# Cached attention on one core: the first V loads moved ahead of K in the load queue, smaller last pieces of wo, and the two output copies exchanged

## The chip, the cores and the metric

The kernel runs on one core of one Trainium2 chip. The metric is the device time of one execution in microseconds (us). A core has five engines: TensorE (PE in the profile; its weight loads are PEld), VectorE (DVE), ScalarE (ACT), GpSimd (POOL) and SyncE (SP), which here only issues transfers. Sixteen DMA engines move the data. A 2 MB load is split over all sixteen, and it has landed when the last of them has finished its share. A landing given without a line of a view is read from the trace's completion counts, sixteen for each load.

## The reference, cut to what matters

```python
# B = 32 batches, 4 queries each, 32 query heads over 4 KV heads, 2048 keys, head size 128, bf16
q = (x @ wq).reshape(B, Sq, Hq, Dh).transpose(0, 2, 1, 3)
scores = einsum("bhqd,bhkd->bhqk", q, repeat(k_cache, 8)) * Dh ** -0.5
o = einsum("bhqk,bhkd->bhqd", softmax(scores), repeat(v_cache, 8))
return o.transpose(0, 2, 1, 3).reshape(B, Sq, Hq * Dh) @ wo
```

Each batch reads 2 MB of K and 2 MB of V once. With wq and wo (8 MB each) that is 151 MB, and little arithmetic on each byte: the time is that of reading.

## The kernel before

All loads go through one list, in one order, from SyncE. There are eight slots of 2 MB in `big`: four for V (slots 0 to 3), three for K (4 to 6), one for another use. The four pieces of wq first lie in the V slots, so no V can be loaded until the q projection has read wq.

```python
NW = 4; LEAD = 3; S2 = 12; VS = 4; KS = 3; LAG = 3
WO = (4, 4, 4, 4, 4, 4, 4, 2, 1, 1)      # heads in each piece of wo; one head is 256 KB

loads = [("k", b) for b in range(LEAD)]
for b in range(B):
    ahead = b + LEAD + (b >= S2)
    ks = [("k", a) for a in range(len(loads) - b, ahead + 1) if a < B]
    loads += ks + [("v", b)]              # K0 K1 K2 | K3 V0 | K4 V1 | K5 V2 ...
# [...]
for kind, b in loads:
    waits = ["qproj"] * (b < VS) if kind == "v" else []
    if kind == "v" and b >= VS:
        waits = [("pv", b - VS)]          # the slot's last V has been used by TensorE
    if kind == "k" and b >= KS:
        waits = [("kt", b - KS, NCH - 1)] # the slot's last K has been transposed by VectorE
    # [...] one DMA of 2 MB on SyncE
```

K3 therefore waits for the transposes of K0, and these come after the q projection. V0 stands behind K3, though all that V0 itself needs is the projection.

At the end the products with wo run piece by piece, and two engines copy the two halves of y out of PSUM, where TensorE has summed them:

```python
for c in range(len(WO)):
    oproj(c)     # per head two matmuls of 128x512, after the wait for piece c
def oproj_out():
    p.op("dve", tensor_copy(y_sb[:, 0:NC], ps_s[:, 0:NC]), [("op", 0)], ("oe", 0))
    p.op("act", activation(y_sb[:, NC:D], ps_s[:, NC:D], ACT.Copy), [("op", 1)], ("oe", 1))
    for j, eng in enumerate(("sp", "act")):
        # [...] eng issues the write of half j after ("oe", j)
```

Of the kernel before, what the change touches and what calls it, by code (L numbers as in the profile page):

```python
# [5 lines left out]
ACT = mybir.ActivationFunctionType  # L6
# [97 lines left out]
def bass_standalone__gqa_block_cached__sampling_kernel(  # L104
# [8 lines left out]
    B, Sq, D = x.shape  # L113
# [11 lines left out]
    NS = 8  # L125
    NW = 4
    LEAD = 3
    S2 = 12
    VS = 4
    KS = 3  # L130
    LAG = 3
    QB = 4
    NC = D // 2
    WO = (4, 4, 4, 4, 4, 4, 4, 2, 1, 1)
    scale = float(Dh) ** -0.5

    x_flat = x.rearrange("b s d -> (b s) d")
# [2 lines left out]
    with ExitStack() as es:  # L140
# [18 lines left out]
        y_sb = P_flat[:, D:2 * D]  # L159
# [8 lines left out]
        ps_s = es.enter_context(nc.psum_tensor("ps_s", [128, Sk], F32))  # L168
# [9 lines left out]
        p = _Program()  # L178
# [7 lines left out]

        loads = [("k", b) for b in range(LEAD)]
        for b in range(B):
            ahead = b + LEAD + (b >= S2)
            ks = [("k", a) for a in range(len(loads) - b, ahead + 1) if a < B]  # L190
            loads += ks + [("v", b)]

        def slot_of(kind, b):
            return b % VS if kind == "v" else VS + b % KS
# [18 lines left out]
        h0 = 0  # L213
        for c, m in enumerate(WO):
            assert h0 // 8 == (h0 + m - 1) // 8
            kind, b = wo_for[h0 // 8]
# [186 lines left out]
        def ot_evac(i):  # L403
            buf = ring_of["ot", i]
            p.op("act", lambda e: e.activation(  # L405
                oT_sb[:, :, :, i * Sq:(i + 1) * Sq].rearrange("p h e s -> p e h s"),
                buf[:, 0:128].rearrange("p (e h s) -> p e h s", e=2, s=Sq), ACT.Copy),
                [("oT", i)], ("ot", i))

        def oproj(c):  # L410
            for h in range(sum(WO[:c]), sum(WO[:c + 1])):
                for j in range(2):
                    out_, lhsT, rhs = ps_s[:, NC * j:NC * (j + 1)], oT_sb[:, h // 2, h % 2, :], wo_at(h, 1)[:, NC * j:NC * (j + 1)]
                    if j == 0:
                        mm = lambda e, a=(out_, lhsT, rhs), h=h: e.matmul(  # L415
                            a[0], lhsT=a[1], rhs=a[2], start=(h == 0), stop=(h == Hq - 1), skip_group_check=True)
                    else:
                        mm = lambda e, a=(out_, lhsT, rhs), h=h: _matmul_held(
                            nc, e, *a, tile_size=(128, 128), tile_position=(0, 0), start=(h == 0), stop=(h == Hq - 1))
                    p.op("pe", mm, [("wo", c), ("ot", B - 1)], ("op", j) if h == Hq - 1 else None)  # L420

        def oproj_out():
            p.op("dve", lambda e: e.tensor_copy(y_sb[:, 0:NC], ps_s[:, 0:NC]), [("op", 0)], ("oe", 0))  # L423
            p.op("act", lambda e: e.activation(y_sb[:, NC:D], ps_s[:, NC:D], ACT.Copy), [("op", 1)], ("oe", 1))  # L424
            for j, eng in enumerate(("sp", "act")):
                p.dma(eng, lambda e, j=j: e.dma_start(out_flat[:, NC * j:NC * (j + 1)], y_sb[:, NC * j:NC * (j + 1)]),
                      [("oe", j)], ("out", j), f"s_o{j}")

# [7 lines left out]
        for i in range(B + LAG):  # L436
            j = i - LAG
# [27 lines left out]
        ot_evac(L)  # L465
        for c in range(len(WO)):
            oproj(c)
        oproj_out()

        p.loop = starts[4:B + 1:4]  # L470
# [55 lines left out]
```

## Time and profile before

| | before |
|---|---|
| median of three runs before the prediction | 365.92 us (365.52 to 366.39) |
| span of the profiled run | 363.9 us |
| moved | 151.7 MB, 417 GB/s over the span |
| busy: TensorE, VectorE, GpSimd, ScalarE | 85%, 76%, 46%, 31% |

The page cuts the span into 40 equal slices. These are the slices of the kernel before, first the DMA engines' busy share in tenths, then what they moved:

```profile
DMA  8999999999999999999999999999999999999994
GB/s 322 432 432 432 391 430 427 427 421 424 429 427 430 430 432 424 423 429 429 430 428 432 428 427 421 429 429 430 430 432 429 425 425 426 429 432 423 403 409 163
```

The stream is full nearly everywhere. Besides the two ends, one slice stands out, the fifth (36 to 45 us, 391 GB/s). This is the timeline of SyncE's queue there; the columns are start, duration, engine and line, operation, destination and source, and the duration is that of the issue, not of the transfer:

```profile
36.05 0.33 SPq L205 DMA_DIRECT2D big<-in_k_cache_dram  x1
36.43 0.43 SPq L205 DMA_DIRECT2D big<-in_v_cache_dram  x1
45.26 0.33 SPq L205 DMA_DIRECT2D big<-in_k_cache_dram  x1
45.62 0.43 SPq L205 DMA_DIRECT2D big<-in_v_cache_dram  x1
```

The first of these is K3. The view of the tile K, narrowed to this one issue, gives its time to landing:

```profile
DMA to landing us min/median/max: 7.7/7.7/7.7
```

So K3 landed at 43.8 us. K2 had landed at 37.88. The regular distance of two 2 MB loads in this trace is 4.89 us, so K3 came 1.04 us late. The windows of 2 us show the same (the last three columns are TensorE's granted clock, the DMA engines' share, and GB/s; a packet is counted where it starts, so a share can exceed 1):

```profile
36.00:38.00 2.00, 2.00 (x11) 0.19 (x2) 1.15 (x2) 0.00 (x0) 0.00 (x0) 1.00 1.14 311
38.00:40.00 2.00, 2.00 (x11) 0.10 (x1) 1.13 (x1) 0.00 (x0) 0.92 (x4) 1.00 0.81 344
```

The chain of work that ended last, in order of time (start, duration, what), shows the tail:

```profile
338.75 18.36 DMA big<-in_wo_dram
357.11 0.05 issue
357.16 0.39 PE ps_s L415
...
360.82 0.60 ACT P_sb L424
```

TensorE's last wait is for the piece of heads 24 to 27, landed at 357.11. From there TensorE alone sets the pace: 16 matmuls, one each 0.216 us. And the last lines of the timeline:

```profile
360.61 0.69 DVE L423 CAST P_sb<-ps_s 128x512 bf16<-128x512 f32 x1 [22.39 <-PE ps_s L415]
360.82 0.60 ACT L424 ACTIVATE P_sb<-ps_s 128x512 bf16<-128x512 f32 x1 [16.26 <-PE ps_s L16]
361.32 0.35 SPq L426 DMA_DIRECT2D out_dram<-P_sb  x1
361.45 0.37 ACTq L426 DMA_DIRECT2D out_dram<-P_sb  x1
```

The first half of y is ready at 360.61 (VectorE starts on it then), 1.02 us after the last byte of wo landed at 359.59. The two writes landed at 363.10 and 363.43.

### The profile page before, as it was taken

Reading aid. Unit: us, or ns where it says so; the run is one execution under the profiler, and the core shown is the slowest. Engines: PE = TensorE matmul, PEld = TensorE weight load, DVE = VectorE, ACT = ScalarE, POOL = GpSimd, SP = SyncE. Lnnn points to the kernel's source line nnn. Section 1 sums busy time; section 2 is a strip of 40 time slices with the busy share of each in tenths; the row PEclk is TensorE's granted clock in tenths of the full one; section 3 lists DMA queues with packets and bytes.
Section 4 is the critical chain, followed back from the end, with each engine's and each line's share of the span. In section 5 each row is a group of like instructions: output and inputs, shape, how many; then the busy total and the mean of one; then the engine's idle time right before and its main releaser. Section 6 shows DMA issues by size and latency. Waiting matters only on the chain. (4 is left out here: it accounts for less than half of the span.)

```text
span 363.9 us, 6546 instructions
## 1 busy us (share of the span) xinstructions
PE 309.2 (85%) x2991; PEld 142.1 (39%) x2402; DVE 275.8 (76%) x275; ACT 111.3 (31%) x142; POOL 165.9 (46%) x261
## 2 busy tenths in 40 slices
PE   1987777899999999998999988888888888989885
PEld 1002000444444444444444444444333334449711
DVE  0028799999999999889999988898888888856100
ACT  1014222333333333333333333333332223333100
POOL 8002155255555555555455544445555555444000
PEclk9999999999999999999999999999999999999999
DMA  8999999999999999999999999999999999999994
GB/s 322 432 432 432 391 430 427 427 421 424 429 427 430 430 432 424 423 429 429 430 428 432 428 427 421 429 429 430 430 432 429 425 425 426 429 432 423 403 409 163
DMA packets 12573, 151.68 MB, mean 417 GB/s; under 512 B 1296, under 2 KB 1552, under 8 KB 3856
## 3 DMA queue, kind: packets, MB, share of 16 engines
q1 hardware_dynamic: 12416, 151.39, 98.5%
q10 hardware_dynamic: 144, 0.13, 0.1%
q8 instruction: 6, 0.10, 0.1%
q14 instruction: 7, 0.06, 0.0%
HBM read 151.26 MB, written 0.26 MB: 416 GB/s over the span
## 5 line engine op out<-in xcount | busy, mean ns | idle before, releaser
L323 DVE STREAM_TRANSPOSE KT_sb<-big 128x1024 f32<-128x1024 f32 x128 | 150.8, 1218 | 10.3 <-DMA big<-in_k_cache_dram 10.3
L350 ACT ACTIVATE P_sb<-ps_s,negmx 128x2048 bf16<-128x2048 f32 x32 | 82.1, 2566 | 86.0 <-DVE negmx L346 86.0
L16 PE MATMUL ps_s<-KT_sb,QD_sb 128*128 128x512 bf16 x384 | 103.7, 377 | 0.0
L372 POOL COPY PD_sb<-PT_sb 32x1024 f32<-32x1024 f32 x62 | 64.2, 1035 | 72.0 <-PE ps_r L383 42.8
L372 POOL COPY big<-PT_sb 32x1024 f32<-32x1024 f32 x61 | 63.7, 1044 | 59.8 <-PE ps_r L383 28.9
L345 DVE TENSOR_REDUCE mx<-ps_s 128x1 f32<-128x2048 f32 x32 | 73.3, 2291 | 10.5 <-PE ps_s L16 9.5
L383 PE MATMUL ps_r<-big 128*128 128x128 bf16 x1024 | 59.8, 219 | 8.7 <-PEq L85 8.6
L383 PE MATMUL ps_r<-big,PD_sb 128*128 128x128 bf16 x1024 | 59.8, 219 | 8.1 <-PEq L85 8.1
L383 PEld LDWEIGHTS ps_r<-big,PD_sb 128*128 128x128 bf16 x1024 | 58.0, 98 | 20.0 <-issue 18.9
L383 PEld LDWEIGHTS ps_r<-big 128*128 128x128 bf16 x1024 | 57.9, 98 | 19.9 <-issue 19.0
L336 PE MATMUL ps_s<-KT_sb,QD_sb 128*128 128x512 bf16 x128 | 48.3, 377 | 17.9 <-PEq L85 17.9
L336 PEld LDWEIGHTS ps_s<-KT_sb,QD_sb 128*128 128x128 bf16 x128 | 12.3, 96 | 103.7 <-issue 103.7
L360 DVE STREAM_TRANSPOSE PT_sb<-P_sb 128x1024 f32<-128x1024 f32 x32 | 39.9, 1246 | 15.1 <-ACT P_sb L350 15.1
L313 POOL COPY QD_sb<-QT_sb 32x64 f32<-32x64 f32 x128 | 29.5, 231 | 38.2 <-DVE QT_sb L292 20.8
L405 ACT ACTIVATE oT_sb<-ps_r 128x128 bf16<-128x128 f32 x32 | 8.9, 278 | 106.6 <-PE ps_r L400 106.6
L16 PE MATMUL ps_r<-QT_sb,ident 128*128 128x512 bf16 x132 | 33.7, 379 | 4.5 <-issue 4.3
L423 DVE CAST P_sb<-ps_s 128x512 bf16<-128x512 f32 x1 | 0.7, 692 | 22.4 <-PE ps_s L415 22.4
L400 PEld LDWEIGHTS ps_r<-ident,o_sb 128*64 128x64 bf16 x128 | 4.6, 109 | 31.2 <-issue 30.9
L390 ACT ACTIVATE o_sb<-ps_r,rinv 128x128 bf16<-128x128 f32 x32 | 11.7, 367 | 15.6 <-PE ps_r L383 13.7
L274 DVE CAST KT_sb<-ps_r 128x512 bf16<-128x512 f32 x2 | 1.3, 685 | 20.1 <-PE ps_r L258 20.1
L415 PE MATMUL ps_s<-big,oT_sb 128*128 128x512 bf16 x30 | 11.4, 380 | 1.6 <-DMA big<-in_wo_dram 1.6
L16 PE MATMUL ps_s<-big,oT_sb 128*128 128x512 bf16 x32 | 12.1, 379 | 0.7 <-ACT oT_sb L405 0.7
(41 smaller groups left out, 86.0 us busy)
## 6 DMA issues: line engine op xcount, KB each, us to landing
big<-in_k_cache_dram SPq DMA_DIRECT2D x32, 2048.0 KB, 17.8
big<-in_v_cache_dram SPq DMA_DIRECT2D x32, 2048.0 KB, 21.5
big<-in_wq_dram SPq DMA_DIRECT2D x4, 2048.0 KB, 14.0
big<-in_wo_dram SPq DMA_DIRECT2D x7, 1024.0 KB, 20.0
big<-in_wo_dram SPq DMA_DIRECT2D x1, 512.0 KB, 17.2
big<-in_wo_dram SPq DMA_DIRECT2D x2, 256.0 KB, 14.8
P_sb<-in_x_dram SPq DMA_DIRECT2D x1, 256.0 KB, 2.7
out_dram<-P_sb SPq DMA_DIRECT2D x1, 128.0 KB, 1.8
```

The source lines that it names most:

```text
L16: return eng.add_instruction(mybir.InstMatmult(name=nc.get_next_instruction_name(), engine=eng.engine, start_tensor_calc=start, stop_tenso ...
L313: p.op("pool", lambda e, s=src, d=dst: e.tensor_copy(d, s), waits if g == 0 else [], ("qd", i) if g == G - 1 else None)
L323: p.op("dve", lambda e, s=src, d=dst: e.transpose(d, s), waits, ("kt", i, c), gives="t_kt" if c == NCH - 1 else None)
L336: mm = lambda e, a_=(out_, lhsT, rhs), f=first, l=last: e.matmul(a_[0], lhsT=a_[1], rhs=a_[2], start=f, stop=l, skip_group_check=True)
L345: p.op("dve", lambda e: e.tensor_reduce(mx[:, i % 4:i % 4 + 1], ps_s[:, :], AX.X, ALU.max), [("qk", i)], ("mx", i))
L350: p.op("act", lambda e: e.activation(P_sb[:, :, :, :].rearrange("p t r w -> p t w r"), ps_s[:, :].rearrange("p (t w r) -> p t w r", w=2, r=R),
L360: p.op("dve", lambda e: e.transpose(dst, src), [("exp", i)] + ([("pd", i - 2, G - 1)] if i > 1 else []), ("pt", i))
L372: p.op("dve" if i >= B - 2 and g < i - B + 4 else "pool", lambda e, s=src, d=dst: e.tensor_copy(d, s), [("pt", i), free], ("pd", i, g))
L383: p.op("pe", lambda e: e.matmul(buf[:, 0:Dh], lhsT=pd_of(i)[:, t // 2, :, :, t % 2].rearrange("p g q -> p (g q)"), rhs=big[:, slot_of("v", ...
L390: p.op("act", lambda e: e.activation(o_sb[:, :], buf[:, 0:Dh], ACT.Copy, scale=rinv[:, i % 4:i % 4 + 1]), [("pv", i), ("rinv", i)] + ([("o ...
L405: p.op("act", lambda e: e.activation(oT_sb[:, :, :, i * Sq:(i + 1) * Sq].rearrange("p h e s -> p e h s"), buf[:, 0:128].rearrange("p (e h ...
L415: mm = lambda e, a=(out_, lhsT, rhs), h=h: e.matmul(a[0], lhsT=a[1], rhs=a[2], start=(h == 0), stop=(h == Hq - 1), skip_group_check=True)
```

## The change

Three small edits: V stands ahead of the next K in the first six batches, so that the queue has work while K3 waits; the last megabyte of wo but one (heads 24 to 27) comes in two pieces, so that TensorE is less behind at the end; and the copies of y are exchanged.

```diff
     LEAD = 3
+    S1 = 6
     S2 = 12
@@
-    WO = (4, 4, 4, 4, 4, 4, 4, 2, 1, 1)
+    WO = (4, 4, 4, 4, 4, 4, 2, 2, 2, 1, 1)
@@
-            loads += ks + [("v", b)]
+            loads += [("v", b)] + ks if b < S1 else ks + [("v", b)]
@@ oproj_out
-            p.op("dve", lambda e: e.tensor_copy(y_sb[:, 0:NC], ps_s[:, 0:NC]), [("op", 0)], ("oe", 0))
-            p.op("act", lambda e: e.activation(y_sb[:, NC:D], ps_s[:, NC:D], ACT.Copy), [("op", 1)], ("oe", 1))
-            for j, eng in enumerate(("sp", "act")):
+            p.op("act", lambda e: e.activation(y_sb[:, 0:NC], ps_s[:, 0:NC], ACT.Copy), [("op", 0)], ("oe", 0))
+            p.op("dve", lambda e: e.tensor_copy(y_sb[:, NC:D], ps_s[:, NC:D]), [("op", 1)], ("oe", 1))
+            for j, eng in enumerate(("act", "sp")):
```

The order becomes K0 K1 K2, V0 K3, V1 K4, V2 K5, V3 K6, V4 K7, V5 K8, then K9 V6 as before.

## The prediction

> **What bounds the kernel now.** The page shows the 16 DMA engines at 0.99 busy or more in almost every fortieth of the span, at 425 to 432 GB/s. The Trainium skill ("HBM Reference", Specifications) gives about 425 GB/s for one core streaming alone; the trace agrees. From 54 us on nearly every 2 MB K or V load lands 4.89 or 4.90 us after the one before. Compute follows. So time can come only from places where the queue is dry, and from what follows the last byte. Three lie near the change:
> 1. Head (queue timeline, windows of 2 us). The loads of wq and K0 to K2 are issued by 4.0 us; K3 waits for K0's transposes and goes out at 36.05, V0 behind it at 36.43. K2 lands at 37.88, K3 at 43.80: 5.93 us instead of 4.89, so 1.04 us lost; windows 36 to 40 show 311 and 344 GB/s. K4, issued at 45.26, lands 0.36 us late likewise.
> 2. Tail (chain of waits). The last wo piece of four heads (24 to 27) lands at 357.11; 16 matmuls of 0.216 us follow, and the first half of y is ready at 360.6. The last piece landed at 359.59, so this is TensorE catching up.
> 3. Output. VectorE copies half 0 (0.69 us, done 361.30, landed 363.10); ScalarE starts half 1 at 360.82 (0.60 us), and its write lands last, at 363.43.
>
> **What the change does.**
> 1. V0 waits only for the q projection (over at about 26.4 us), so it is queued before K2 has landed. K3 is issued at 36.05 as before, now behind 4.9 us of V0: the gap closes, and each later pair has one V more ahead of it. Worth about 1.0 us (0.7 to 1.3: the 16 engines lost 0.72 to 1.03 us each at K3, 0.05 to 0.37 at K4). The price: K3 to K8 stand one V later, about 3.9 us net. Before, K8 landed 4.7 us ahead of its first transpose; about 0.8 is left, so VectorE may wait a little. As loads set the pace, that costs nothing unless the queue runs dry.
> 2. Heads 24 and 25 would land at about 355.83, 26 and 27 at 357.11, 28 and 29 at 358.33, the last as before. TensorE starts its last eight matmuls at 358.38, not at about 358.89: 0.5 us off. No bytes are added; one more issue on a queue 15 us ahead is free.
> 3. The later half gets the slower copy (+0.09 us) but the quicker write (1.78 us from issue to landing against 1.98), the earlier half the reverse: about 0.1 us off.
>
> All three lie on the critical path: 1.0 + 0.5 + 0.1 = 1.6 us, estimated from these durations. 365.92 - 1.6 = 364.3 us, range 363.4 to 365.3. Chances: faster by over 2% 0.02, within 2% 0.97, slower 0.01.
>
> **What would show it right.** V0's issue near 26.6 us; K2, V0, K3 landing 4.9 us apart; all later landings about 1 us earlier; windows 36 to 40 at about 425 GB/s. At the end, TensorE's last wait on wo is for heads 28 and 29, and the first half is done about 1.8 us after they land.
>
> **What would make it wrong.** V in front of K starving VectorE around K5 to K8, so that slots free late and the queue runs dry; single DMA engines held up elsewhere (V1 landed 1.31 us late before, beside an instruction fetch at 57 us), which moves the end by a microsecond either way; or the engine that ends last having lost least in the gap.

## The result, and the profile after

| | before | after |
|---|---|---|
| median, six runs each | 365.87 us (365.52 to 366.84) | 364.33 us (364.26 to 364.40) |
| ratio | | 0.9954 (95%: 0.9941 to 0.9967) |
| the same later, on another chip | 366.20 us (365.95 to 367.30) | 364.43 us (364.33 to 364.63) |
| ratio | | 0.9944 (95%: 0.9929 to 0.9958) |

A ratio is the mean time of one kernel's runs over that of the other's of the same rounds, so it is not quite the ratio of the medians. The verdict is "same" at the 2% line; the gain is about half a per cent, and clear. Not only the middle moved: the kernel before spreads over 1.3 us in both series, the changed one over 0.1 to 0.3 us.

The slices of the changed kernel; the fifth now moves 434 GB/s:

```profile
DMA  7999999999999999999999999999999999999995
GB/s 324 432 430 434 434 423 423 427 430 430 423 425 427 430 430 424 430 425 430 430 426 427 424 432 432 425 427 427 430 432 425 427 427 431 430 427 427 401 407 195
```

SyncE's queue, from 20 us on. V0 goes out at 26.82, nine microseconds ahead of K3:

```profile
26.82 0.33 SPq L206 DMA_DIRECT2D big<-in_v_cache_dram  x1
35.97 0.33 SPq L206 DMA_DIRECT2D big<-in_k_cache_dram  x1
36.34 0.43 SPq L206 DMA_DIRECT2D big<-in_v_cache_dram  x1
45.17 0.33 SPq L206 DMA_DIRECT2D big<-in_k_cache_dram  x1
```

K3's time to landing, in the same narrowed view, and the windows:

```profile
DMA to landing us min/median/max: 11.6/11.6/11.6
```

```profile
36.00:38.00 2.00, 2.00 (x11) 0.19 (x2) 1.07 (x1) 0.00 (x0) 0.00 (x0) 1.00 1.04 442
38.00:40.00 2.00, 2.00 (x11) 0.10 (x1) 1.22 (x1) 0.00 (x0) 0.93 (x4) 1.00 0.94 401
```

K2 landed at 37.78, V0 at 42.67, K3 at 47.57: 4.89 and 4.90 us apart. K3 waits longer in the queue, and nothing waits for K3. The mean of the two windows is 421 GB/s, against 327 before.

The chain now ends with the piece of heads 28 and 29, and eight matmuls behind it:

```profile
341.77 15.61 DMA big<-in_wo_dram
357.38 0.04 issue
357.42 0.39 PE ps_s L416
...
359.36 0.69 DVE P_sb L425
```

```profile
359.14 0.60 ACT L424 ACTIVATE P_sb<-ps_s 128x512 bf16<-128x512 f32 x1 [15.56 <-PE ps_s L416]
359.36 0.69 DVE L425 CAST P_sb<-ps_s 128x512 bf16<-128x512 f32 x1 [22.14 <-PE ps_s L16]
359.77 0.37 ACTq L427 DMA_DIRECT2D out_dram<-P_sb  x1
360.08 0.35 SPq L427 DMA_DIRECT2D out_dram<-P_sb  x1
```

The last byte of wo landed at 358.62 and the writes at 361.56 and 361.91. The two traces divide the 1.52 us between the last landings of the output (363.43 and 361.91) like this:

| stretch | before | after | gain |
|---|---|---|---|
| start to K2's landing (not touched) | 37.88 | 37.78 | 0.10 |
| K2's landing to wo's last landing | 321.71 | 320.84 | 0.87 |
| to the first half of y ready | 1.02 | 0.52 | 0.50 |
| to the last landing of the output | 2.82 | 2.77 | 0.05 |

### The profile page after: what moved, and what is told of

It is laid out like the page before. It is cut to its first block, busy times and chain, and to the rows that moved or that the text cites. A ratio compares the mean times of both kernels' runs of the same rounds, so it can differ in the third digit from the quotient of the medians. Undisturbed runs are those within 1.5% of the kernel's fastest.

```text
span 362.4 us, 6547 instructions
## 1 busy us (share of the span) xinstructions
PE 309.1 (85%) x2991; PEld 142.1 (39%) x2402; DVE 275.8 (76%) x275; ACT 111.4 (31%) x142; POOL 166.1 (46%) x261
```

## The experiments

The theory at the outset (A): the stream of loads sets the pace; the spot at K3 is pure loss, as is TensorE's lag at the end; each part of the change can be added up. Rivals: later hold-ups hide the gap; VectorE starves on a later K; the gain comes from the output. Every experiment gave a correct result. "Before" in the table is the kernel before, 11 runs.

| kernel | median (range) of 6 | before | ratio (95%) |
|---|---|---|---|
| e1_order | 364.88 (364.75 to 365.04) | 366.73 (365.66 to 367.66) | 0.9950 (0.9931 to 0.9969) |
| e2_pieces | 365.64 (365.15 to 366.85) | same | 0.9973 (0.9950 to 0.9996) |
| e3_out | 366.50 (365.63 to 367.37) | same | 0.9996 (0.9973 to 1.0019) |
| e4_one_v | 365.33 (364.99 to 365.63) | same | 0.9964 (0.9945 to 0.9984) |
| after_again | 364.43 (364.33 to 364.63) | 366.20 (365.95 to 367.30) | 0.9944 (0.9929 to 0.9958) |
| e5_two_v | 365.48 (364.98 to 366.26) | same | 0.9974 (0.9957 to 0.9991) |
| e7_coarse | 365.68 (365.48 to 365.78) | same | 0.9977 (0.9962 to 0.9991) |
| e8_wo8k | 364.02 (363.91 to 364.36) | same | 0.9933 (0.9918 to 0.9948) |
| e9_three_v | 364.96 (364.65 to 365.18) | 366.26 (365.48 to 367.84) | 0.9962 (0.9941 to 0.9983) |
| e6_all_v | 366.62 (366.42 to 368.07) | same | 1.0017 (0.9992 to 1.0041) |

### e1_order: the load order alone

```diff
# to the kernel before
+    S1 = 6
-            loads += ks + [("v", b)]
+            loads += [("v", b)] + ks if b < S1 else ks + [("v", b)]
```

> The kernel before with only the load order changed (V ahead of the next K for the first six batches). Theory A (the stream of loads sets the pace, and the dry spot of 1.04 us at K3 is pure loss): K3's landing is 9.8 us behind K2's, all later loads land about 0.9 us earlier, the tail keeps its 3.5 us from the piece of heads 24 to 27 to the first half: 0.9 us faster (0.7 to 1.1). Rival B (the engine that ends last is decided by later hold-ups, and the gap is absorbed by its slack): under 0.4 us faster. Rival C (K one V later starves VectorE): no gain or a loss, and VectorE's wait for K clearly above 10.3 us.

Measured: 1.84 us faster in the mean (366.73 to 364.89), more than theory A allowed; its 95% interval, 1.1 to 2.5 us, begins where the range of theory A ends. Rivals B and C are out: the gain is not under 0.4 us, and VectorE's waits for K fell to 9.0 us in all. The surprise is the spread. All six runs lie within 0.3 us, while the kernel before, on the same chip, spreads over 2.0 us, with its quickest run only 0.8 us behind e1_order's median. So the order takes away a loss that differs from run to run, and the trace of the kernel before had shown a small one.

### e2_pieces: the wo pieces alone

```diff
# to the kernel before
-    WO = (4, 4, 4, 4, 4, 4, 4, 2, 1, 1)
+    WO = (4, 4, 4, 4, 4, 4, 2, 2, 2, 1, 1)
```

> The kernel before with only the smaller wo pieces. Theory A: the landings up to the last one stay as they are, and the first half of y is ready 0.52 us behind the last landing instead of 1.02: 0.5 us faster (0.35 to 0.65). Rival: the extra DMA and the two more waits of TensorE eat it, under 0.2 us.

Measured: 0.94 us in the mean, with an interval of 0.1 to 1.8 us, too wide to tell 0.5 from 0.2, since this kernel keeps the old load order, with which the time varies from run to run (here over 1.7 us). The trace decides: the last byte landed at 360.38, the first half was ready at 360.89, 0.51 us later, as foreseen.

### e3_out: the output's engines alone

```diff
# to the kernel before: the edit of oproj_out shown above, nothing else
```

> The kernel before with only the output's engines exchanged. Prediction's view: 0.1 us faster, as the later half gets the quicker write. What the two traces suggest (from the first half ready to the last landing 2.82 us before, 2.77 after): 0.05 us, below what these runs can tell from nothing. Rival: half or more of the 1.5 us came from here; then 0.5 us or more faster.

Measured: 0.9996, nothing that can be told. The rival of half the gain is out. The two traces above also correct a reason. The prediction took ScalarE's write for the slower one (1.98 us to landing against SyncE's 1.78). After the exchange ScalarE's took 1.79 and SyncE's 1.83. So ScalarE's write is not slower as such: it took 1.98 us as the second of two writes issued 0.13 us apart. No run has SyncE's write second at that distance.

### e4_one_v: only V0 moved ahead

```diff
# to e1_order
-    S1 = 6
+    S1 = 1
```

> As e1_order, but only V0 moved ahead (S1 = 1). Theory A with a lead: an issue that comes less than about 3 us before the previous load has landed leaves the engines dry. K3 is covered by V0, but K4, issued at 45.2 us, then stands behind K3's landing at 47.6, a lead of 2.4 us, and loses 0.2 to 0.7 us: the gain is only 0.3 to 0.7 us. Rival: closing the first gap is all there is to it, and one V gives the same 0.9 us as six.

Measured: 1.40 us faster in the mean, 365.33 us, spread 0.6 us. In the trace K3 lands on time (4.90 us after V0), and the windows from 36 to 40 show 442 and 401 GB/s. But K4, issued at 45.23 us, lands 5.20 us after K3, 0.31 late, inside the 0.2 to 0.7 expected. Against e1_order, 0.44 us are missing. The rival (one V is as good as six) is out. The expected size against the kernel before (0.3 to 0.7 us) was again too small, for the same reason as in e1_order.

### after_again: the whole change, on the chip of the next three

No edit to the changed kernel.

> The whole change once more, beside the kernel before and on the chip of the next three. The first four experiments showed that the kernels in which K3 comes late (before, e2_pieces, e3_out) spread over 1.7 to 2 us from run to run, and those in which V0 stands ahead over 0.3 us (e1_order) and 0.6 us (e4_one_v). Theory D: the dry spot does not cost a fixed 1.04 us; restarting 16 drained engines costs 1.4 to 2.6 us, different in each run, and that is what the order removes. Then this kernel has a spread under 0.3 us at about 364.3 us, and the mean gain is 1.7 to 2.3 us, more than the 1.6 us predicted. Theory A with a fixed loss: 1.5 us, and the spread of the kernel before is the chip's own, so this one shares it.

Measured: 364.43 us, spread 0.30 us (just not under 0.3), 2.04 us faster in the mean (95%: 1.5 to 2.6). The interval begins where theory A's 1.5 us stands, so the mean gain alone hardly tells D from A. The spread tells more: a spread of the chip's own is out, since the kernel before spreads over 1.35 us on the same chip in the same rounds, and a loss that varies, as in theory D, fits. Whether the parts add up cannot be told to better than this interval: the means of e1_order, e2_pieces and e3_out sum to 2.9 us, with 0.5 us from the trace for the wo pieces to some 2.5 us.

### b_again: the kernel before, looked at once more

No edit to the kernel before.

> The kernel before, unchanged, looked at once more: how much do K3 and K4 land behind the regular 4.89 us this time? In three traces with the same head so far it was 1.04 + 0.36 (before), 1.74 + 0.89 (e2_pieces) and 1.41 + 0.88 us (e3_out). Theory D (the restart of drained engines costs a different time in each run): again between 1.0 and 2.6 us in all, and a run over 366.5 us shows over 2 us. Rival (the spread comes from elsewhere): the same 1.40 us here whatever the time.

Measured: one run of 367.32 us. K3 lands 0.98 us late behind K2 (5.87 us) and K4 0.25 us late (5.15), 1.23 us in all. That clause of theory D failed: a slow run was to show over 2 us. But K2's landing itself was late, at 39.50 us. This is TensorE's timeline at the head, first the earlier trace of the kernel before, then this one:

```profile
8.65 0.58 PE L258 MATMUL ps_r<-big,P_sb 128*128 128x512 bf16 x1 [4.05 <-DMA big<-in_wq_dram]
```

```profile
10.29 0.58 PE L258 MATMUL ps_r<-big,P_sb 128*128 128x512 bf16 x1 [5.74 <-DMA big<-in_wq_dram]
```

The first piece of wq came 1.6 us later. By the completion counts in the trace, fifteen DMA engines had delivered their share by 8.57 us and one at 10.15. The projection waits for all sixteen, so everything behind it moved: K3 was issued at 37.69 instead of 36.05, and now the other fifteen engines had nothing to do. The windows of this run:

```profile
36.00:38.00 2.00, 1.16 (x6) 0.19 (x2) 2.00 (x3) 0.00 (x0) 0.00 (x0) 1.00 0.50 213
38.00:40.00 2.00, 2.00 (x11) 0.19 (x2) 0.79 (x1) 0.00 (x0) 0.00 (x0) 1.00 0.90 180
```

So the loss at K3 has two sources that vary: the restart (1.04, 1.74 and 1.41 us in three traces that issue K3 within 0.1 us of each other), and any late engine at the head, whose delay the gap hands to all sixteen. The last byte of wo landed at 361.00 here, 1.41 us later than in the first trace, close to the 1.44 us between the two times. The landing tells of the last engine only. In the mean of the sixteen engines K3 and K4 together came 0.84, 1.26, 1.08 and 2.31 us late in before, e2_pieces, e3_out and b_again, which orders the four times (365.88, 366.19, 366.63 and 367.32 us) once e2_pieces' 0.5 us of shorter tail are added back. With V0 ahead, a projection 1.6 us late would put V0's issue at about 28.4 us, still some 5 us before it must be out (K2's end at 37.8 less the lead of 4.1 us that e9_three_v shows below to be enough). No trace of the changed kernel has such a late engine, so this is an argument and not shown.

### e5_two_v and e5_again: V0 and V1 moved ahead

```diff
# to e1_order
-    S1 = 6
+    S1 = 2
```

> The kernel before with V0 and V1 moved ahead (S1 = 2), nothing else. With two V ahead K3 and K4 are both covered; K5, issued at about 54.1 us, then stands 3.3 us ahead of the landing in front of it. Theory D and A with a lead of 3 us: as e1_order, 364.9 us, spread under 0.4 us. Rival: each V moved adds something, and the time lies between e4_one_v (365.33) and e1_order (364.88).

> e5_two_v once more, for a look: its first trace fell on a quick run (365.16 of 364.98 to 366.26) and shows K5's dry spot (3.2 us between K5's issue and K4's landing on 15 of the engines) hidden behind one engine that an instruction fetch had held back. Theory D: the engines' share of busy time dips in the 56 to 58 us stretch again, and if the time is above 365.5 us, K5 lands over 0.3 us late on the engine that ends last. Rival: no dip, and the spread of e5_two_v is of another source.

Measured: 365.48 us, spread 1.3 us, no better than one V. Both the theory's 364.9 us and the rival's place between e4_one_v and e1_order missed (though on different chips). The trace of e5_two_v has a new thin spot at K5, issued at 54.06 us, 3.3 us before 15 of the 16 engines had finished K4 (57.3). Its windows (two from the trace of e5_two_v, then the same two of e1_order, where V1 is in the queue):

```profile
56.00:58.00 2.00, 2.00 (x11) 0.10 (x1) 1.74 (x2) 0.00 (x0) 1.88 (x3) 1.00 1.01 401
58.00:60.00 2.00, 2.00 (x10) 0.00 (x0) 1.97 (x3) 0.87 (x1) 1.34 (x5) 1.00 0.93 393
```

```profile
56.00:58.00 2.00, 2.00 (x11) 0.10 (x1) 1.74 (x2) 0.00 (x0) 1.88 (x3) 1.00 1.09 451
58.00:60.00 2.00, 2.00 (x10) 0.00 (x0) 1.97 (x3) 0.76 (x1) 1.47 (x5) 1.00 1.02 434
```

The second look (365.48 us) has 401 GB/s in the first window again, so the spot is there in both. Both fell on runs of middling time or better, and in both the spot is hidden at K5 itself by one engine that an instruction fetch had held back. The thin spot is shown; that it makes the whole spread of 1.3 us is not.

### e9_three_v: V0 to V2 moved ahead

```diff
# to e1_order
-    S1 = 6
+    S1 = 3
```

> The kernel before with V0, V1 and V2 moved ahead (S1 = 3). The first load behind the change of order is K6, issued at about 63 us, some 4.2 us before the landing in front of it, against 3.2 for K5 in e5_two_v, which still dried up. If 4 us are enough, spread under 0.4 us at 364.9 us as e1_order; if not, between e5_two_v and e1_order: 365.0 to 365.5 us.

Measured: 364.96 us, within 0.1 us of e1_order on the same chip; the spread, 0.5 us, is above the 0.4 foreseen. K6, issued at 63.20 us, stands 4.1 us ahead of 15 engines' end of K5 (67.3), and the windows from 64 to 68 show 459 and 434 GB/s. So this lead was enough, and 3.3 us in e5_two_v was not. But 3.9 us, counted the same way, was not enough for K4 in e2_pieces (issued at 45.20, V0 done on 15 engines at 49.13, K4 0.88 us late): there the engines had come apart, and the first was done with V0 at 47.73. Counted to the first engine's end of the load in front, all traces agree: leads of up to 3.0 us lost 0.4 us or more, summed over the engines, and those of 3.1 to 3.9 us (K5 of e4_one_v at 3.1, K6 here at 3.7) not over 0.25. How much is lost does not follow from the lead alone: 0.6 us at 2.7 (K4 of the kernel before), 1.9 at 3.0 (K5 of e5_two_v).

### e7_coarse: the opposite of the second part

```diff
# to the changed kernel
-    WO = (4, 4, 4, 4, 4, 4, 2, 2, 2, 1, 1)
+    WO = (4, 4, 4, 4, 4, 4, 4, 4)
```

> The changed kernel with all wo pieces of four heads, the opposite of the change's second part. If the tail is TensorE's work behind the piece it waits for last, then eight matmuls of 0.216 us stand behind the last landing: the first half is ready about 1.75 us after it instead of 0.52, so 1.2 us slower than the changed kernel, about 365.5 us. Rival: larger packets and fewer issues make the last landing so much earlier that it evens out (the last landing more than 0.6 us earlier).

Measured: 1.22 us slower in the mean than the changed kernel of the same rounds (365.67 and 364.45). The last byte landed at 358.61, as there; the rival is out. From the timeline:

```profile
358.66 0.39 PE L416 MATMUL ps_s<-big,oT_sb 128*128 128x512 bf16 x1 [0.55 <-DMA big<-in_wo_dram]
...
360.38 0.60 ACT L424 ACTIVATE P_sb<-ps_s 128x512 bf16<-128x512 f32 x1 [16.72 <-PE ps_s L416]
```

The first half is ready 1.77 us after the last byte: eight matmuls at 0.216 us and the way to ScalarE. The tail is the work behind the piece that is waited for last.

### e6_all_v: V ahead of K to the end

```diff
# to the changed kernel
-    S1 = 6
+    S1 = 32
```

> The changed kernel with V ahead of the next K in all 32 batches (S1 = 32). K then stands 4.9 us later for good; from K9 or K10 on its landing falls behind the moment when VectorE wants it. The prediction named this as the price. Theory (loads set the pace, slots come free early enough): VectorE waits more for K than 8.8 us in all, yet the queue does not dry up, and the time is the changed kernel's 364.4 us within 0.3 us. Rival (the first six are a limit that matters): VectorE's waits delay the slots, the queue dries up, 1 us or more slower.

Measured: 366.62 us, 2.2 us slower than the changed kernel's 364.43 (of another chip). Each side was half right: the time is the rival's (over 1 us slower), but not for its reason. The queue did not dry up: the last byte landed at 358.82, 0.2 us from the changed kernel's. But VectorE waits twice as long for K (line of the waits: who, for what, total, times, longest; first the kernel before, then the changed kernel, then this one),

```profile
DVE KT_sb L323 <- DMA big<-in_k_cache_dram: 10.3, 13, 1.0
```

```profile
DVE KT_sb L324 <- DMA big<-in_k_cache_dram: 8.8, 11, 0.9
```

```profile
DVE KT_sb L324 <- DMA big<-in_k_cache_dram: 17.8, 17, 1.1
```

and the chain that ended last holds no DMA at all:

```profile
by line: PE ps_s L416 1.9%; PE ps_s L16 1.9%; DVE P_sb L425 0.2%; ACT oT_sb L406 0.1%; PE ps_r L401 0.1%; issue 0.1%
```

TensorE begins the products with wo at 347.69 us instead of 343.94 and has 64 matmuls of 0.216 us before it, 13.8 us, which reach past the last landing. Loads set the pace only as long as the compute is not pushed behind their end; K's place in the queue does that.

### e8_wo8k: a version that beats both

```diff
# to the changed kernel (its core; oT_sb becomes [128, Hq // 4, 4, NT])
-        wo_v = wo.rearrange("(h p e) n -> p h (e n)", p=128, e=2)
+        wo_v = wo.rearrange("(h p e) n -> p h (e n)", p=128, e=4)
-                dst = wo_at(h0, m).rearrange("p (h n) -> p h n", n=2 * D)
-                src = wo_v[:, h0 // 2:(h0 + m) // 2, :]
+            dst, src = wo_at(h0, m), wo_v[:, h0 // 4, h0 % 4 * D:(h0 % 4 + m) * D]
@@ pe_ot
-            for e_ in range(2):
-                for u in range(2):
-                    out_ = buf[64 * u:64 * (u + 1), 64 * e_:64 * (e_ + 1)]
+            for e_ in range(4):
+                for u in range(4):
+                    out_ = buf[32 * u:32 * (u + 1), 32 * e_:32 * (e_ + 1)]
```

> A try at something better: the changed kernel with wo's rows dealt to the partitions four at a time and not two, so that a piece of four heads has runs of 8 KB instead of 4 KB (and the transposition of o is done in sixteen small matmuls instead of four). In the trace a 2 MB load of 16 KB runs takes 4.89 us, and 1 MB of wo in 4 KB runs 2.56 us; from both, an estimate: about 9.5 ns a run beside 27.2 GB/s an engine, so 2.48 us with 8 KB runs. Six such pieces save 0.46 us: about 363.9 us. Rival: the run length does not matter and wo is slow for another reason, such as reading with gaps; then no gain, or a loss from the twelve added small matmuls in each batch.

Measured: 0.38 us faster in the mean than the changed kernel of the same rounds (364.07 and 364.45; only the slowest of its six runs, 364.36, reaches into the other's range, 364.33 to 364.63). Pieces of 1 MB land 2.47 to 2.49 us apart instead of 2.56, and from V31's landing to the last of wo it takes 19.96 us instead of 20.38. The rival of gaps is out by this kernel's own pieces of two heads: they have runs of 4 KB with gaps of 4 KB between them and land 1.28 us apart, as the changed kernel's do, which have no gaps. So the run length was the reason, and the small matmuls cost nothing that can be seen. Against the kernel before it is 2.43 us in the mean, 0.7%.

## Why the prediction was right, and where it was not

The predicted 364.3 us met the measured 364.33, and "within 2%" was right. Point by point:

- **The bound.** Right. In the mean of the sixteen engines every K and V load after K2 came 0.80 to 0.84 us earlier, and the end with them. The landings, each set by the engine that is last just then, came 1.1 to 1.5 us earlier until V16 and 0.93 to 0.99 from there on (V31's from 339.22 to 338.24).
- **V0 closes the gap.** Right in mechanism: V0 out at 26.82 us (26.6 foretold), K2, V0 and K3 4.89 and 4.90 us apart, 421 GB/s from 36 to 40 us (425 foretold).
- **Its size, "about 1.0 us (0.7 to 1.3)".** Right for the trace it was read from (0.87 us), too small for the kernel. e1_order gained 1.84 us in the mean. A single trace had shown one draw of a loss that varies: in four traces of this head K3 and K4 together came 1.40, 2.63, 2.29 and 1.23 us late, the last with a late start on top. That the total still came out is luck, as a small loss was taken off a quick time: the 365.92 us it started from, the median of the three runs known then, lies near the quick end (11 runs in each of the three later calls have medians of 366.73, 366.20 and 366.26), and the trace came from those quick runs too (365.88 us).
- **"The queue is dry".** Only partly the right word. In the first trace the engines count as busy in that stretch (shares 1.14 and 0.81) at three quarters of the bytes: K3's first packets began at 37.0 us, as K2's ran out, and most took 1.2 to 1.7 us each instead of 0.61. A load that comes late starts slowly. In b_again, where K3 was later still, the engines did stand idle. The Trainium skill ("Perfetto Trace Analysis", DMA Instruction — HWDGE) says that descriptors are generated at issue and that a DMA engine may begin before all are there; a slow first packet would fit engines that wait for descriptors, but no run here shows the descriptors, so that stays open.
- **The price in K's place.** Right for six: VectorE waited 8.8 us for K, not more than before (10.3). Its reason, that such waits cost nothing unless the queue runs dry, is wrong in general. e6_all_v lost 2.2 us with a full queue.
- **The wo pieces, 0.5 us.** Right: 1.02 to 0.52 us in the traces, TensorE's last wait is for heads 28 and 29, and the first half is ready 1.76 us after they landed (1.8 foretold). e7_coarse confirms the term from the other side, 1.2 us foretold and 1.22 measured.
- **The output, 0.1 us.** Between 0.05 us in the traces and nothing that can be measured; the reason given (ScalarE's write is slower) was wrong.
- **What would make it wrong.** The hold-ups of single engines are there: in the changed kernel K4 landed 6.31 us after V1, beside an instruction fetch at 56.6 us, like V1 before. The Trainium skill ("DMA: Bandwidth & Descriptors", Queues, rings and completion order) says that a DMA is split over up to sixteen rings and that each engine consumes its own in order. The trace agrees: the engine held back keeps its lag, no other takes over its share, and at the last piece of wo the first engine was done at 356.36 and the last at 358.62. These 2.3 us (2.4 in the kernel before) are untouched by the change.

Left open: what makes the restart cost 1.04 us in one run and 1.74 in another; what held one engine back in b_again; and the rest of e5_two_v's spread.

## What to carry to other kernels

In a kernel bound by loads, put into the queue, in front of each load that must wait, one that need not, early enough: here an issue 3.1 us before the first DMA engine was done with the load in front was early enough and 3.0 us was not, a distance that belongs to these loads of 2 MB. Look at the spread of the runs as well as at one trace: a thin spot in the stream shows there, since it hands on every delay that happens before it. Do not carry the reordering further than the gap needs; an order that is good at the head can leave the compute behind the last byte at the end.

## What the Trainium skill lacked or had wrong

- "DMA: Bandwidth & Descriptors" (Latency and other measured facts) has about 600 ns to the first byte. The first packet of x began at 1.77 us, 0.65 us after its issue ended and 1.03 after it began, which agrees if counted from the end. It lacks how long a 2 MB load takes from there to the full rate: the first packets of the late K3 mostly took 1.2 to 1.7 us instead of 0.61, an issue 1.4 to 3.0 us before the first engine was done with the load in front left a loss, and one 3.1 to 3.9 us before it did not.
- The same page (Specifications) gives 512 B as the least for full rate, and works out its cost per packet for small descriptors only. Here runs of 4 KB took 2.56 us per MB, runs of 8 KB 2.48, runs of 16 KB 2.45 (half of 4.89), so some 4.5% between 4 and 16 KB.
- "Runtime: NRT & Kernel Launch" (Instruction fetch mechanics) says that instructions come in blocks of 16 KiB over the sequencer's own DMA queue, and calls the cost of a block's boundary mostly hidden. The block's size agrees (six such packets in each trace, seven in e8_wo8k). In a stream of loads the cost is not hidden: beside the block fetched at 56.6 us one of sixteen engines came 1.4 us late with K4 (57.37 for the fifteenth engine, 58.77 for the last), and the lag stays with that engine. In every trace the load beside this fetch is late by 1.7 to 2.1 us, summed over the engines; in e2_pieces and e3_out its landing is not, as another engine was last there. That the fetch causes it is inferred from the time alone; no run took the fetch away.
- "HBM Reference" (Specifications) has about 425 GB/s for a core streaming alone. The slices agree or stand a little higher, up to 434.
